# A transformer block on one core: the bound's root in a query and a key part, norms over the whole array, values transposed between score tiles

## The chip, the cores and the metric

The kernel runs on one core of a Trainium2 chip. The metric is the device time of one execution in microseconds (us); lower is better. The median of three runs of the kernel before is 1413.35 us, the runs lie between 1410.28 and 1417.75 us. Its profile comes from one more execution.

Five engines work side by side, each through its own instructions in order: TensorE (PE; PEld is its loading of weights), VectorE (DVE), ScalarE (ACT), GpSimd (POOL) and SyncE (SP), which here only issues DMAs. An engine that waits for a semaphore holds up everything that stands behind it in its own order.

## The reference

2048 tokens of width 512 go through a block of two parts: attention with 32 query heads of width 16, which share one key and one value head, and a gated feed-forward part of inner width 1792.

```python
def _A_ref(x, wq, wk, wv, wo):
    B, S, D = x.shape
    H = 32
    Dh = D // H
    q = (x @ wq).reshape(B, S, H, Dh).transpose(0, 2, 1, 3)
    k = x @ wk
    v = x @ wv
    scores = jnp.einsum("bhqd,bkd->bhqk", q, k) * (Dh ** -0.5)
    p = _softmax(scores, axis=-1)
    o = jnp.einsum("bhqk,bkd->bhqd", p, v)
    return o.transpose(0, 2, 1, 3).reshape(B, S, H * Dh) @ wo

def _B_ref(x, w_gate, w_up, w_down):
    return (_gelu(x @ w_gate) * (x @ w_up)) @ w_down

h = x + _A_ref(_layernorm(x), ...)
h2 = h + _B_ref(_layernorm(h), ...)
```

## The kernel before

The 2048 tokens are cut into four blocks of 512 (NB = 4, T = 512). Matrix products run in about full precision: each operand is split into a high and a low part, and three products (high by high, high by low, low by high) are added up.

**The prologue** (`prologue`, up to 50 us) normalizes the 16 tiles of 128 tokens, turns them on TensorE (`turn`), and projects keys and values of each block together (`project_k`, tiles pk). From a block's tile `add_k` writes the keys into `kaug`, `leave_k` copies the tile into SBUF as `vT`, `low_k` forms the keys' low part on GpSimd, `turn_v` transposes the values on TensorE (four transposes of 128x128, tile pv) and `leave_v` copies them into `v_sb` on VectorE. Beside that `project_q` projects the queries of block 0 in four chunks of 8 heads: chunk 0 in the generator `q_first`, chunks 1 to 3 in `q_rest`. Each chunk's tile pq is split into `qh` and `ql` (two buffers of each), and SP writes them to DRAM (`q_d`) in three DMAs, from where tiles of four heads (`qg`) are read.

**The bound.** In place of the row maximum the softmax subtracts a bound: with a head's query norms and the largest key norm, a line that lies above their product. `norm_k` sums the squares of a block's keys with a matmul against `ones`; `max_k` takes the largest; `k2m` is the maximum over the four blocks. `norm` does the same for the queries of a chunk with the matrix `sel`, with `q2` its largest value per head. `factors` makes the line's two coefficients out of q2 and k2m in four small GpSimd steps, ScalarE forms the tile `m` from them, and `first_bound` sends its rows into `qg_first` and to DRAM. The chunk for which this is urgent is chunk 0 of block 0.

**The steps.** Then the loop in `run` goes through score steps n. A step (`score`, `scores`) multiplies one block of 128 keys with the queries of two heads, a pair of matmuls into a PSUM tile s of two banks, and ScalarE takes the exponential of the whole tile. Two steps make one i of four heads; `finish` then weighs the values (`weigh`, four matmuls into acc). In the first steps three s tiles take six banks and acc one; the eighth bank is the only one left to `psum1` there (width = 1). From step START = 8 on, projections of the later query blocks are mixed in (line 429).

**What sets the order.** The pools and a hand-kept order: TensorE, ScalarE and GpSimd run in the order in which the code issues, and VectorE and SP do so in the prologue's end and in the steps. Behind step 2 the loop drains what is left of `q_rest`: for chunk 3 that is the split of the copy `pq_raw` into qh and ql on VectorE (lines 129 and 130), its square (line 265) and its three writes on SP (line 270). Its qh takes the buffer of chunk 1.

Lines of the profile that matter: L223 projection of block 0's queries, L242 the copy pq_raw, L280 norm of the queries, L290 to L299 the factors, L323 the tile m, L354 to L386 the DMAs of the first query tile and of m, L431 scores, L435 exponentials, L439 weighing, L1361 norm of the keys, L1387 the values' transposes, L1392 and L1393 their copies, L1464 k2m.

Of the kernel before, what the change touches and what calls it, by code (L numbers as in the profile page):

```python
# [9 lines left out]
F32 = mybir.dt.float32  # L10
# [20 lines left out]
W2 = 3  # L31

AHEAD_W = 2

LAST_Q = 258

# [26 lines left out]
def kernel(  # L63
# [104 lines left out]
    def run(outer, first):  # L168
# [37 lines left out]
        def project_q(b, cs, eng, col, whole=None):  # L206
# [68 lines left out]
                    yield 3  # L275

            def norm():
                pn = psum1(f"pqn_{b}_{cs[0]}")[:H, :]
                for i, c in enumerate(cs):
                    nc.tensor.matmul(  # L280
                        pn, sel[:, c, :], qss[i], start=(i == 0), stop=(i == len(cs) - 1)
                    )
                qn = eb.tile([H, T], F32, tag="qn", bufs=1, name=f"qn_{b}_{cs[0]}")
                nc.vector.tensor_copy(qn, pn)
                nc.vector.tensor_reduce(q2[:, col : col + 1], qn, axis=AX.X, op=ALU.max)

                mm = eb.tile([H, 3], F32, tag="mm", bufs=2, name=f"mm_{b}_{cs[0]}")

                def factors():
                    nc.gpsimd.tensor_scalar(  # L290
                        mm[:, 0:1], q2[:, col : col + 1], k2m, 1e-30, op0=ALU.mult, op1=ALU.add
                    )
                    nc.gpsimd.tensor_tensor(
                        mm[:, 1:2], mm[:, 0:1], power[:H, 0:1], op=ALU.pow
                    )
# [3 lines left out]
                    nc.gpsimd.tensor_scalar(  # L299
                        mm[:, 1:2], mm[:, 1:2], k2m, 0.5, op0=ALU.mult, op1=ALU.mult  # L300
                    )

                m = eb.tile([H, T], F32R, tag="m", bufs=2, name=f"m_{b}_{cs[0]}")

                def bound():
                    factors()
                    nc.gpsimd.tensor_scalar(
                        m, qn, mm[:, 1:2], mm[:, 2:3], op0=ALU.mult, op1=ALU.add
                    )
                    hs = slice(cs[0] * HC, (cs[-1] + 1) * HC)  # L310
                    nc.gpsimd.dma_start(q_d[hs, 3 * DH, tsl].bitcast(F32), m[hs].bitcast(F32))

                if not urgent:
                    after.append([2, bound])
                return qn, mm, m, factors

            if not urgent:
                norms.append(norm)
# [8 lines left out]


        after, squares, norms, pause = [], [], [], [0]
        ms = {}  # L330
# [64 lines left out]
        if first:  # L395
            set_banks("ps_pro")
            width = 8
            order = tc.manual_schedule(engines={mybir.EngineType.DVE})
            with order:
                qg_first = prologue(  # L400
                    psum1, xT, wq_hi, wq_lo, sel, k2m, q_first, q_rest, advance,
                    first_q, first_bound, fill_first, eb
                )
        sb = outer.enter_context(tc.tile_pool(name="attn", bufs=1, side="right"))
# [669 lines left out]
        with tc.manual_schedule(engines={mybir.EngineType.SP, mybir.EngineType.DVE}):  # L1074
# [6 lines left out]
            while n < lead:  # L1081
# [33 lines left out]
                for kind in kinds:  # L1115
                    if kind == "m" and not rest and not held and token not in (None, REST):
                        held = token[1] == 1
                        tokens = token, next(work)
                        score(n, [(lane, step) for lane, _, step in tokens])
                        token = next(work, None)  # L1120
                        left -= 2
                    else:
                        score(n)
                    n += 1
                if first and n == 2:
                    for _ in q_rest:
                        pass
# [117 lines left out]
        late.close()  # L1245


    def prologue(psum1, xT, wq_hi, wq_lo, sel, k2m, q_first, q_rest, advance, first_q, first_bound, fill_first, eb):
        with ExitStack() as pro:
            sb = pro.enter_context(tc.tile_pool(name="pro", bufs=1))  # L1250
            xT[0] = [sb.tile([P, DC, T], F32R, name=f"xT_{w}_0") for w in ("hi", "lo")]
# [25 lines left out]
            def repeat_k():  # L1277
# [17 lines left out]
                out=sel, in_=sel, compare_op=ALU.is_ge, fill=0.0, base=DH - 1,  # L1295
                pattern=[[-P, DC], [DH, H]], channel_multiplier=-1,
            )

            bias = sb.tile([P, 1], F32, name="bias")
            nc.vector.memset(bias, 0.0)  # L1300
# [1 line left out]
            nc.vector.memset(neg, -1.0)  # L1302
            for r0 in (0, 64):
                nc.scalar.dma_start(bias[r0 + 3 * DH : r0 + KR, :], neg)
            ones = sb.tile([DH, H], BF16, name="ones")
            nc.vector.memset(ones, 1.0)
            k2 = sb.tile([H, NB], F32, name="k2")
            nc.vector.memset(v_sb, 1.0)

# [42 lines left out]
                    )  # L1352

            def square_k(b, pk):
                ks = sb.tile([DH, T], BF16, tag="ks", bufs=2, name=f"ks_{b}")
                nc.scalar.activation(ks, pk[:DH, :], AF.Square)
                return ks

            def norm_k(b, ks):
                pn = psum1(f"pkn_{b}")[:H, :]  # L1360
                nc.tensor.matmul(pn, ones, ks, start=True, stop=True)  # L1361
                return pn

            def max_k(b, pn):
                nc.vector.tensor_reduce(k2[:, b : b + 1], pn, axis=AX.X, op=ALU.max)
# [100 lines left out]
            with tc.manual_schedule(engines={mybir.EngineType.SP}):  # L1466
# [100 lines left out]
```

## Time and profile before

| what | value |
|---|---|
| median of the runs | 1413.35 us |
| span of the profiled execution, first to last instruction | 1408.1 us |
| TensorE busy | 1391.7 us, 99% of the span |
| ScalarE busy | 1041.2 us, 74% |
| VectorE busy | 552.7 us, 39% |
| GpSimd busy | 189.4 us, 13% |
| mean granted TensorE clock | 0.996 |
| HBM read and written | 142.93 and 49.55 MB |

The profiled execution is known by its span; what lies around the span is not in the profile, and the runs were timed apart from it. The rows in the prediction come from these views: the page (span, busy time by engine), the busy time by stretches of the span with the granted clock (1.00 is full speed), the waits (who waited for whom), and the instructions of one engine in order of time. In the last, a row gives the start and the length in us, the engine and the source line, the operation, the written tile and the read ones, the shape, and the count of instructions merged into it; brackets hold the idle time ahead of it and what ended that. A merged row runs from its first start to its last end. Matmuls overlap in these rows, so that distances between starts tell the rate.

### The profile page before, as it was taken

The page shows a single profiled execution, that of the slowest core. Times are in us where ns is not written, and L with a number is a line of the kernel's source. Part 1 is how long each engine was busy: PE and PEld are TensorE (multiplying, and loading weights), DVE is VectorE, ACT ScalarE, POOL GpSimd, SP SyncE. Part 2 cuts the span into 40 slices and gives each one's busy share as a digit, 9 for nine tenths or more (in the row PEclk, how much of TensorE's full clock was granted, in tenths as well). Part 3 has the DMA queues.
Part 4 walks back from the last instruction along what each step waited for, and adds up shares of the span by engine and source line. Part 5 has one row for each costly group of instructions (what it writes and reads, how often), then busy time and mean ns, then how long its engine had stood idle before and what let it go on. Part 6 is the DMA issues. An engine that isn't in the chain of part 4 may idle for free.

```text
span 1408.1 us, 25648 instructions
## 1 busy us (share of the span) xinstructions
PE 1391.7 (99%) x10646; PEld 782.7 (56%) x10646; DVE 552.7 (39%) x982; ACT 1041.2 (74%) x1149; POOL 189.4 (13%) x288
## 2 busy tenths in 40 slices
PE   8999999999999999999999999999999999999998
PEld 7433333335555555555555655555555555557886
DVE  7322323333342434333252433424352342427665
ACT  7699999996777787777787777777787777772000
POOL 6655565501000000000000000001000000002000
PEclk9999999999999999999999999999999999999999
DMA  4578777842341322233252332223242241335551
GB/s 160 162 238 273 236 243 243 298 134 91 126 150 53 124 106 102 73 112 122 84 169 72 117 118 87 87 100 111 99 151 97 88 147 56 134 124 198 181 199 59
DMA packets 85041, 194.52 MB, mean 138 GB/s; under 512 B 9904, under 2 KB 24240, under 8 KB 84884
## 3 DMA queue, kind: packets, MB, share of 16 engines
q1 hardware_dynamic: 77484, 167.39, 35.3%
q0 software_dynamic: 7264, 25.30, 5.0%
q8 instruction: 86, 1.41, 0.4%
q14 instruction: 39, 0.32, 0.1%
q10 hardware_dynamic: 168, 0.10, 0.0%
HBM read 142.93 MB, written 49.55 MB: 137 GB/s over the span
## 4 chain that ended last, share of the span: by engine, by line
PE 93%; ACT 3%; DMA 1%; issue 1%; DVE 1%; POOL 0%; SPq 0%; ACTq 0%; DVEq 0%; POOLq 0%
PE acc L439 33%; PE s L431 19%; PE pu L949 9%; PE pg L949 8%; PE pd L949 4%; PE pq L429 4%; PE pd L626 3%; ACT p L435 3%; PE pd L648 3%; PE pg L648 3%; PE pu L648 3%; PE pp L626 2%; PE pp L757 1%; DMA x<-in_A_x_dram 1%; PE pxt L693 1%
## 5 line engine op out<-in xcount | busy, mean ns | idle before, releaser
L435 ACT ACTIVATE p<-s 128x1024 f32<-128x1024 f32 x1024 | 969.7, 1030 | 224.6 <-PE s L431 220.1
L439 PE MATMUL acc<-p,v_sb 128*32 128x512 f32 x4096 | 496.4, 600 | 0.0
L431 PE MATMUL s<-qg,kaug 50*128 50x512 f32 x1984 | 416.3, 423 | 3.7 <-ACT p L435 3.6
L431 PEld LDWEIGHTS s<-qg,kaug 50*128 50x128 f32 x1984 | 194.6, 184 | 217.8 <-ACT p L435 120.6
L439 PEld LDWEIGHTS acc<-p,v_sb 128*32 128x32 f32 x4096 | 109.8, 109 | 229.2 <-issue 226.0
L949 PE MATMUL pu<-x2h,w 64*128 64x512 f32 x672 | 211.8, 391 | 0.0
L949 PE MATMUL pg<-x2h,w 64*128 64x512 f32 x672 | 211.5, 391 | 0.1
L949 PEld LDWEIGHTS pu<-x2h,w 64*128 64x128 f32 x672 | 115.8, 185 | 15.1
L949 PEld LDWEIGHTS pg<-x2h,w 64*128 64x128 f32 x672 | 116.2, 185 | 12.6 <-DVE g L823 0.5
L949 PE MATMUL pg<-x2l,w 64*128 64x512 f32 x336 | 122.2, 391 | 0.0
L949 PE MATMUL pu<-x2l,w 64*128 64x512 f32 x336 | 121.8, 390 | 0.0
L826 ACT ACTIVATE ga<-ga 128x512 f32<-128x512 f32 x56 | 35.3, 634 | 89.2 <-DVE ga L821 89.2
L139 POOL TENSOR_SCALAR rstd<-mv 128x1 f32<-128x1 f32 x16 | 3.5, 221 | 666.4 <-DVE mv L137 666.4
L949 PE MATMUL pd<-w,gh 64*128 64x512 f32 x384 | 81.3, 392 | 0.0
L891 DVE TENSOR_TENSOR h<-h,pd 128x512 f32<-128x512 f32 x48 | 31.9, 685 | 115.4 <-PE pd L949 66.4
L1192 DVE SCALAR_TENSOR_TENSOR ga<-ga,g 128x512 f32<-128x512 f32 x70 | 48.3, 691 | 52.3 <-ACT ga L826 51.2
L452 DVE COPY oT<-acc 128x512 f32<-128x512 f32 x32 | 22.1, 692 | 112.1 <-PE acc L439 111.9
L479 DVE RECIPROCAL oc<-oc 128x128 f32<-128x128 f32 x64 | 56.3, 921 | 24.3 <-DMA oc<-acc_d 19.5
L810 DVE COPY g<-pg 128x512 f32<-128x512 f32 x56 | 38.8, 692 | 62.8 <-PE pg L949 57.0
L949 PEld LDWEIGHTS pu<-x2l,w 64*128 64x128 f32 x336 | 57.9, 185 | 7.6
L949 PEld LDWEIGHTS pg<-x2l,w 64*128 64x128 f32 x336 | 58.1, 185 | 6.1
L823 DVE SCALAR_TENSOR_TENSOR g<-g,pu 128x512 f32<-128x512 f32 x56 | 38.2, 683 | 40.4 <-PE pu L949 30.4
(248 smaller groups left out, 1462.4 us busy)
## 6 DMA issues: line engine op xcount, KB each, us to landing
w<-w_d SPq DMA_DIRECT2D x112, 512.0 KB
w<-w_d SPq DMA_DIRECT2D x28, 1024.0 KB
qg<-q_d SPq DMA_DIRECT2D x46, 200.0 KB
q_d<-qh SPq DMA_DIRECT2D x32, 256.0 KB
wo<-wo_d SPq DMA_DIRECT2D x8, 1024.0 KB
acc_d<-oT SPq DMA_DIRECT2D x31, 256.0 KB
oc<-acc_d SPq DMA_DIRECT2D x124, 64.0 KB
w_d<-w_0b POOLq DMA_DIRECT2D x14, 512.0 KB, 7.6
```

The lines of the kernel that those rows point to most:

```text
L429: step()
L431: nc.tensor.matmul(s[:, a, :], kaug[rows, kc * P : (kc + 1) * P], qg[rows, 2 * u + a, :], start=True, stop=True,)
L435: nc.scalar.activation(p[:, 2 * u : 2 * u + 2, :], s, AF.Exp, scale=SCALE)
L439: nc.tensor.matmul(acc[32 * j : 32 * j + 32, :], v_sb[:, kc, :], p[:, j, :], start=(kc == 0), stop=(kc == KC - 1), skip_group_check=True,)
L479: nc.vector.reciprocal(oc[:, 1, sl], oc[:, 1, sl])
L626: nc.tensor.matmul(banks[k], lhsT[rows], rhs[rows], start=(turn == 0 and i == 0), stop=(turn == 1 and i == n - 1), skip_group_check=True,)
L648: nc.tensor.matmul(bank, lhsT, rhs, start=(i == 0), stop=(i == len(ts) - 1))
L810: nc.vector.tensor_copy(g, pg)
L823: nc.vector.scalar_tensor_tensor(g, g, 0.5, pu, op0=ALU.mult, op1=ALU.mult)
L826: nc.scalar.activation(a, a, AF.Tanh, scale=GELU_A * GELU_C)
L949: nc.tensor.matmul(e["bank"], lhsT[rows], rhs[rows], start=i == 0 and not e["both"], stop=last and e["both"], skip_group_check=True,)
L1192: (soon or lazy).pop(0)()
```

## The change

Four things are changed, all in the prologue and the first steps.

The root of the urgent bound is split: `norm` computes the query part (`ab`: half the root, and half its inverse, of q2) on GpSimd as soon as q2 is there; `first_factors` then needs of k2m only its root, on GpSimd, and one product on VectorE.

The norms' matmuls of the prologue use all 128 columns and rows: `ones` becomes a 128x128 matrix with zeros behind the first 16 rows, the keys' squares are taken over all 128 rows, and the urgent query norm multiplies with a new 128x128 matrix `wide` (the first chunk's columns of `sel`, zeros elsewhere). The results are read from the same 32 partitions.

The values of blocks 2 and 3 are no longer transposed in the prologue, but behind steps 3 and 4 of the loop (TURN_V), into the bank of `psum1`.

Behind steps 2, 5 and 6 (BUSY) stand three matmuls each whose results nobody reads, into the same bank.

```diff
+TURN_V = {3: 2, 4: 3}
+
+BUSY = (2, 5, 6)
...
             def norm():
-                pn = psum1(f"pqn_{b}_{cs[0]}")[:H, :]
+                pn = psum1(f"pqn_{b}_{cs[0]}")
                 for i, c in enumerate(cs):
                     nc.tensor.matmul(
-                        pn, sel[:, c, :], qss[i], start=(i == 0), stop=(i == len(cs) - 1)
-                    )
+                        pn if urgent else pn[:H, :], wide[0] if urgent else sel[:, c, :],
+                        qss[i], start=(i == 0), stop=(i == len(cs) - 1),
+                    )
+                pn = pn[:H, :]
...
+                if urgent:
+                    ab = eb.tile([H, 2], F32, name="ab")
+                    nc.gpsimd.tensor_scalar(
+                        mm[:, 0:1], q2[:, col : col + 1], 1e-30, None, op0=ALU.add
+                    )
+                    nc.gpsimd.tensor_tensor(
+                        ab[:, 0:1], mm[:, 0:1], power[:H, 0:1], op=ALU.pow
+                    )
+                    nc.gpsimd.tensor_scalar(
+                        ab[:, 1:2], mm[:, 0:1], ab[:, 0:1], 0.5, op0=ALU.mult, op1=ALU.mult
+                    )
+                    nc.gpsimd.tensor_scalar(ab[:, 0:1], ab[:, 0:1], 0.5, None, op0=ALU.mult)
+
+                def first_factors():
+                    nc.gpsimd.tensor_tensor(mm[:, 0:1], k2m, power[:H, 1:2], op=ALU.pow)
+                    nc.vector.tensor_scalar(mm[:, 1:3], ab, mm[:, 0:1], None, op0=ALU.mult)
...
+                    if first and n in TURN_V:
+                        turn_last(TURN_V[n])
+                    if first and n in BUSY:
+                        bank = psum1(f"busy_{n}")
+                        for _ in range(3):
+                            nc.tensor.matmul(
+                                bank, kaug[:KR, :P], cur["qg"][:KR, 0, :],
+                                start=True, stop=True,
+                            )
...
+            wide.append(sb.tile([P, P], BF16, name="wide"))
+            nc.gpsimd.memset(wide[0], 0.0)
+            nc.gpsimd.tensor_copy(wide[0][:, :H], sel[:, 0, :])
...
-            ones = sb.tile([DH, H], BF16, name="ones")
-            nc.vector.memset(ones, 1.0)
+            ones = sb.tile([P, P], BF16, name="ones")
+            nc.vector.memset(ones, 0.0)
+            nc.vector.memset(ones[:DH], 1.0)
...
-                ks = sb.tile([DH, T], BF16, tag="ks", bufs=2, name=f"ks_{b}")
-                nc.scalar.activation(ks, pk[:DH, :], AF.Square)
+                ks = sb.tile([P, T], BF16, tag="ks", bufs=2, name=f"ks_{b}")
+                nc.scalar.activation(ks, pk, AF.Square)
...
                 advance(q_rest, 12)
-                for b in range(1, NB):
-                    leave_v(b, turn_v(b, vTs[b]))
+                leave_v(1, turn_v(1, vTs[1]))
                 advance(q_rest, 3 * DC * (DC - FIRST_Q) - 21)
-            return qg
+            return qg, lambda b: leave_v(b, turn_v(b, vTs[b]))
```

On TensorE, from the end of the queries' projection (pq) to the first mixed one, the score pairs (s), the weighing (acc) and the last of the projection stand before as follows; the three groups pv ahead of them are the transposes of blocks 1, 2 and 3.

```order
L1387 MATMUL pv_748<-ident,vT_651 128x128 x4
L1387 MATMUL pv_755<-ident,vT_688 128x128 x4
L1387 MATMUL pv_762<-ident,vT_691 128x128 x4
...
L431 MATMUL s_0_816<-qg_first,kaug 128x512 x2
L431 MATMUL s_1_820<-qg_first,kaug 128x512 x2
L431 MATMUL s_0_834<-qg_first,kaug 128x512 x2
L431 MATMUL s_1_838<-qg_first,kaug 128x512 x2
L431 MATMUL s_0_846<-qg_first,kaug 128x512 x2
L431 MATMUL s_1_850<-qg_first,kaug 128x512 x2
L439 MATMUL acc_0_814<-p_815,v_sb 32x512 x4
```

The same place of TensorE now, from the first score pair to the first weighing:

```order
L453 MATMUL s_0_809<-qg_first,kaug 128x512 x2
L453 MATMUL s_1_813<-qg_first,kaug 128x512 x2
L1152 MATMUL busy_817<-qg_first,kaug 128x512 x3
L453 MATMUL s_0_831<-qg_first,kaug 128x512 x2
L1422 MATMUL pv_835<-ident,vT_697 128x128 x4
L453 MATMUL s_1_842<-qg_first,kaug 128x512 x2
L1422 MATMUL pv_846<-ident,vT_700 128x128 x4
L453 MATMUL s_0_857<-qg_first,kaug 128x512 x2
L1152 MATMUL busy_861<-qg_first,kaug 128x512 x3
L453 MATMUL s_1_865<-qg_first,kaug 128x512 x2
L1152 MATMUL busy_869<-qg_first,kaug 128x512 x3
L461 MATMUL acc_0_807<-p_808,v_sb 32x512 x4
```

The transposes of blocks 2 (pv_835) and 3 (pv_846) moved behind the third and the fourth score pair, and nine matmuls (busy) were added.

On VectorE, before, the copies of the values (v_sb) of blocks 1, 2 and 3 stand together, ahead of the splits of query chunks 2 (ql_2) and 3 (qh_3, ql_3, qs_3):

```order
L1392 COPY v_sb<-pv_748 128x4x14
L1393 COPY v_sb<-pv_748 128x4x2
L1392 COPY v_sb<-pv_755 128x4x14
L1393 COPY v_sb<-pv_755 128x4x2
L1392 COPY v_sb<-pv_762 128x4x14
L1393 COPY v_sb<-pv_762 128x4x2
L130 TENSOR_TENSOR ql_2_773<-pq_2_738,qh_2_772 128x512
L265 TENSOR_TENSOR qs_2_776<-qh_2_772 128x512
L129 CAST qh_3_824<-pq_raw_3_794 128x512
L130 TENSOR_TENSOR ql_3_825<-pq_raw_3_794,qh_3_824 128x512
L265 TENSOR_TENSOR qs_3_828<-qh_3_824 128x512
```

The same place of VectorE now:

```order
L1427 COPY v_sb<-pv_755 128x4x14
L1428 COPY v_sb<-pv_755 128x4x2
L134 TENSOR_TENSOR ql_2_766<-pq_2_745,qh_2_765 128x512
L269 TENSOR_TENSOR qs_2_769<-qh_2_765 128x512
L133 CAST qh_3_821<-pq_raw_3_787 128x512
L134 TENSOR_TENSOR ql_3_822<-pq_raw_3_787,qh_3_821 128x512
L269 TENSOR_TENSOR qs_3_825<-qh_3_821 128x512
L1427 COPY v_sb<-pv_835 128x4x14
L1428 COPY v_sb<-pv_835 128x4x2
L1427 COPY v_sb<-pv_846 128x4x14
L1428 COPY v_sb<-pv_846 128x4x2
```

The copies of blocks 2 and 3 moved behind the split of query chunk 3.

More of the change, by code (lines that the diff above doesn't have):

```diff
@@ L314, in norm @@
                     after.append([2, bound])
-                return qn, mm, m, factors
+                return qn, mm, m, first_factors if urgent else factors
             if not urgent:
@@ L329, in run @@
         after, squares, norms, pause = [], [], [], [0]
-        ms = {}
+        ms, wide = {}, []
         q_first = project_q(0, range(FIRST_Q), nc.scalar, 0)
@@ L399, in run @@
             with order:
-                qg_first = prologue(
-                    psum1, xT, wq_hi, wq_lo, sel, k2m, q_first, q_rest, advance,
+                qg_first, turn_last = prologue(
+                    psum1, xT, wq_hi, wq_lo, sel, k2m, wide, q_first, q_rest, advance,
                     first_q, first_bound, fill_first, eb
@@ L1245, in run, with prologue @@
         late.close()
-    def prologue(psum1, xT, wq_hi, wq_lo, sel, k2m, q_first, q_rest, advance, first_q, first_bound, fill_first, eb):
+    def prologue(psum1, xT, wq_hi, wq_lo, sel, k2m, wide, q_first, q_rest, advance, first_q, first_bound, fill_first, eb):
         with ExitStack() as pro:
@@ L1354, in square_k @@
             def square_k(b, pk):
-                ks = sb.tile([DH, T], BF16, tag="ks", bufs=2, name=f"ks_{b}")
-                nc.scalar.activation(ks, pk[:DH, :], AF.Square)
+                ks = sb.tile([P, T], BF16, tag="ks", bufs=2, name=f"ks_{b}")
+                nc.scalar.activation(ks, pk, AF.Square)
                 return ks
             def norm_k(b, ks):
-                pn = psum1(f"pkn_{b}")[:H, :]
+                pn = psum1(f"pkn_{b}")
                 nc.tensor.matmul(pn, ones, ks, start=True, stop=True)
-                return pn
+                return pn[:H, :]
             def max_k(b, pn):
```

## The prediction

> **What bounds the kernel now.** I read the page, then busy time by stretches around the clock's dips, then each engine in order of time between 35 and 62 us. The page first:
>
> ```profile
> span 1408.1 us, 25648 instructions
> PE 1391.7 (99%) x10646; PEld 782.7 (56%) x10646; DVE 552.7 (39%) x982; ACT 1041.2 (74%) x1149; POOL 189.4 (13%) x288
> ```
>
> TensorE is busy in 99% of the span. What the change can win or lose lies in the few stretches where it waits or where its clock is low. In busy time by stretches, the columns are the length, the busy time of PE, PEld, DVE, ACT and POOL, then the granted clock, the DMA share and GB/s:
>
> ```profile
> 49.94:53.35 3.41, 1.93 (x10) 0.79 (x8) 0.00 (x0) 2.21 (x3) 3.35 (x7) 1.00 0.67 188
> 53.35:56.76 3.41, 2.91 (x12) 0.77 (x12) 0.00 (x0) 3.41 (x5) 3.26 (x3) 0.50 0.54 170
> 56.76:60.17 3.41, 3.41 (x16) 0.70 (x12) 1.72 (x3) 2.52 (x3) 2.55 (x4) 0.50 0.52 190
> 60.24:310.00 249.76, 249.67 (x1891) 93.81 (x1887) 71.32 (x101) 244.55 (x263) 127.46 (x162) 1.00 0.75 241
> 310.00:1395.00 1085.00, 1080.79 (x8440) 644.74 (x8437) 438.71 (x786) 755.73 (x824) 21.70 (x44) 1.00 0.33 115
> ```
>
> In 49.94 to 53.35 us TensorE worked 1.93 of 3.41 us, and for the next 6.82 us it was granted half its clock. From 60.24 us it has full clock and 0.09 us of idle in 250 us. So an instruction that comes some microseconds later at 60 us is still as late at 310 us. Behind 310 us the idle is 4.2 us in all, and its waits are of this kind (engine, line, what it waited for, us in total, times, longest):
>
> ```profile
> PE s L431 <- ACT p L435: 3.6, 14, 0.4
> ```
>
> These 14 waits are for ScalarE, which follows TensorE; they move along and absorb nothing. I therefore take a shift at 60.24 us, where the first mixed projection starts, to reach the end in full. TensorE around the place (start, length, line, operands, count, idle before):
>
> ```profile
> 45.36 1.47 PE L1387 MATMUL pv<-ident,vT 128*128 128x128 f32 x12
> 48.31 0.40 PE L223 MATMUL pq<-xT_lo,wq_hi 128*128 128x512 f32 x1
> 48.54 0.39 PE L223 MATMUL pq<-xT_hi,wq_lo 128*128 128x512 f32 x1
> 49.94 0.39 PE L223 MATMUL pq<-xT_hi,wq_lo 128*128 128x512 f32 x1
> 51.08 1.03 PE L431 MATMUL s<-qg_first,kaug 50*128 50x512 f32 x6 [0.75 <-ACT pq_raw L242]
> 52.81 0.50 PE L431 MATMUL s<-qg_first,kaug 50*128 50x512 f32 x2 [0.70 <-ACT p L435]
> 53.73 1.71 PE L431 MATMUL s<-qg_first,kaug 50*128 50x512 f32 x4 [0.41 <-ACT p L435]
> 55.37 1.93 PE L439 MATMUL acc<-p,v_sb 128*32 128x512 f32 x8
> 57.23 1.22 PE L431 MATMUL s<-qg_first,kaug 50*128 50x512 f32 x4
> 58.38 1.93 PE L439 MATMUL acc<-p,v_sb 128*32 128x512 f32 x8
> 60.24 0.50 PE L429 MATMUL pq<-xT_hi,wq_hi 64*128 64x512 f32 x1
> ```
>
> Three gaps (0.75, 0.70, 0.41 us) precede and accompany the dip. ScalarE in the same time:
>
> ```profile
> 45.78 0.81 ACT L323 ACTIVATE m<-qn,mm 32x512 fp32r<-32x512 f32 x1 [2.00 <-POOL mm L299]
> 50.43 0.60 ACT L242 ACTIVATE pq_raw<-pq 128x512 f32<-128x512 f32 x1 [1.86 <-PE pq L223]
> 51.73 5.61 ACT L435 ACTIVATE p<-s 128x1024 f32<-128x1024 f32 x6 [0.71 <-PE s L431]
> 61.02 11.37 ACT L435 ACTIVATE p<-s 128x1024 f32<-128x1024 f32 x12 [1.01 <-PE s L431]
> ```
>
> The first score tile waits for the copy pq_raw, which ends at 51.03 us. An exponential takes 0.94 us (5.61 over 6).
>
> **The start (memsets, the wide matrix).** GpSimd gets a memset and a small copy behind its selects:
>
> ```profile
> 1.82 0.31 POOL L1294 TENSOR_SCALAR_AFFINE_SELECT sel<-sel 128x128 bf16<-128x128 bf16 x1
> 5.11 0.23 POOL L1320 TENSOR_SCALAR rstd<-mv 128x1 f32<-128x1 f32 x1 [2.97 <-DVE mv L1318]
> ```
>
> A wait of 2.97 us covers both; without that cover they would cost two operations of about 0.3 us. VectorE's one extra memset comes to 0.1 us at most; I take nothing.
>
> **Norms in whole-array form.** Five matmuls get 128 columns of weights for 32, and the key squares 128 rows for 16. The weight loads (idle before in brackets):
>
> ```profile
> 35.90 0.09 PEld L1361 LDWEIGHTS <-ones 16*32 16x32 bf16 x1 [0.17 <-issue]
> 36.21 0.19 PEld L1349 LDWEIGHTS pk<-xT_hi,wk_hi 128*128 128x128 f32 x1 [0.23 <-issue]
> ```
>
> Between a 32-column load (0.09 us) and a 128-column one (0.19 us) lies 0.1 us, so five cost 0 to 0.5 us; a gain is excluded as no work goes away. TensorE is busy without a gap from here to 50.34 us, so this would count on the way to the first score. I take 0.4 us, near the 128-column row.
>
> **The root in two parts.** GpSimd's old chain and VectorE's inputs to it:
>
> ```profile
> 43.80 0.26 POOL L290 TENSOR_SCALAR mm<-q,k2m 32x1 f32<-32x1 f32 x1 [6.66 <-DVE k2m L1464]
> 44.13 0.54 POOL L293 TENSOR_TENSOR mm<-mm,power 32x1 f32<-32x1 f32 x1
> 45.12 0.62 POOL L299 TENSOR_SCALAR mm<-mm,k2m 32x1 f32<-32x1 f32 x1
> 42.07 0.67 DVE L285 TENSOR_REDUCE q<-qn 32x1 f32<-32x512 f32 x1
> 43.55 0.14 DVE L1464 TENSOR_SCALAR k2m<-k2m 32x1 f32<-32x1 f32 x1
> 43.62 0.67 DVE L129 CAST qh<-pq 128x512 fp32r<-128x512 f32 x1
> ```
>
> Before, four steps ran behind k2m, 43.80 to 45.74 us. Now four start behind the query maximum (42.74 us) and take 1.0 us for scale and root and about 0.7 for the two small ones: to 44.45 us. Then come the key's root (0.54) and one VectorE product (0.14), so m can start at 45.3 instead of 45.78 us: 0.5 us earlier. VectorE waits in that product for GpSimd's root, and the split of query chunk 1, queued behind it, starts near 45.25 instead of 43.62 us and ends near 47.2 us (three operations of 0.67). SP fetches that chunk only behind the rows of m:
>
> ```profile
> 46.62 1.49 SPq L381 DMA_DIRECT2D qg_first<-m  x2
> 48.71 0.68 SPq L270 DMA_DIRECT2D q_d<-qh  x1
> 50.20 2.05 SPq L270 DMA_DIRECT2D q_d<-qh  x2
> ```
>
> SP reaches it at 48.71 us, so the slip is hidden. The 0.5 us gained on m is about what the norms lose, so I leave SP's writes where they are; the bounds are 0.5 us earlier and unchanged.
>
> **Two transposes moved, nine matmuls added.** Eight transposes of 0.12 us leave the stretch before the first score, which therefore starts near 50.5 us (51.08 less 1.0, plus 0.4). Blocks 2 and 3 are now transposed behind the third and fourth score pair. There only one PSUM bank is left for such tiles: the dummies and both transposes share it. The transposes of block 3 must wait until VectorE has copied out block 2, and that copy now stands behind the split of query chunk 3. VectorE's rows:
>
> ```profile
> 46.00 0.22 DVE L1392 COPY v_sb<-pv 128x56 f32<-128x56 f32 x1 [0.38 <-PE pv L1387]
> 46.13 0.16 DVE L1393 COPY v_sb<-pv 128x8 f32<-128x8 f32 x1
> 58.29 0.43 DVE L129 CAST qh<-pq_raw 128x512 fp32r<-128x512 f32 x1 [8.41 <-DMA q_d<-qh]
> 59.36 0.69 DVE L265 TENSOR_TENSOR qs<-qh 128x512 bf16<-128x512 f32 x1
> ```
>
> The split reuses the buffer of chunk 1 and waits 8.41 us for SP's write of it, issued at 50.20, to land at 58.29 us. Before, nobody waited for that. Now TensorE does: after the fourth score pair, near 53.2 us, it stands in order at block 3's transposes with every later score, dummy and weighing behind it.
>
> The sum, step by step:
> - VectorE is free of the split at 60.05 us (59.36 + 0.69), the two copies take 0.29 (46.00 to 46.29): bank free 60.34, TensorE goes on at 60.4.
> - TensorE idles some 7 us, more than in the stretch that halved the clock before, so it restarts at half clock.
> - Work left ahead of the first mixed projection, at half clock: four transposes 2 x 0.49 = 0.98; four score pairs at 0.61 (1.22 over 2) = 2.44; six dummies at 2 x 0.23 (48.31 to 48.54) = 2.76; two weighings at 1.93 = 3.86. Together 10.04 us, or 5.02 at full clock.
> - The clock came back at 60.17 us behind a stretch of 3.41 us in which TensorE never paused, and had not come back behind one with 2.91 of 3.41. One full stretch behind 60.4 us ends between 63.8 and 67.2 us, by where its edge falls. Work done at T + (10.04 - (T - 60.4))/2: 67.1 to 68.8 us.
> - Against 60.24 us that is 6.9 to 8.6 us later; the middle is 7.7. Landing 0.5 us earlier takes off 0.25.
>
> The Trainium skill, "TensorE: Matmul & The Clock Gate", Part 1, has a free-running window of about 3.4 us and lets one busy window restore the clock; an estimate by it alone gives the same 3.4 to 6.8 us of half clock after the restart. Its table of practical rules allows pauses up to about 3 us without a loss. The trace differs there: the pauses of at most 0.75 us at 50 to 54 us were followed by half clock. By that rule dummies of this kind would buy nothing here; by the rows they might, but the stall of 7 us is beyond either.
>
> Scale: the profiled execution gives its span, 1408.1 us; the median of the runs, 1413.35, lies 5.25 above it, which is what lies around the span and the scatter (1410.28 to 1417.75). I add the difference of spans to the median: 1413.35 + 7.7 = 1421.0 us. About 0.5% (7.1 us) is what a measurement of this kernel can tell from no change.
>
> **The rivals.**
> - *The bank is free in time (not slower).* If block 2's copies were done by 53.2 us, for which chunk 1's write would have to land by 51 us, TensorE would need from 50.5 us eight pairs at 0.34 (1.03 over 3), nine dummies at 0.23, eight transposes at 0.12 and two weighings at half of 1.93: 7.7 us, to 58.2, and the exponentials 0.6 + 8 x 0.94 = 8.1, to 58.6 against 61.02. Gain 2.0 to 2.4, say 2.2: 1411.1 us. For it: the clock would not dip. Against it: the landing at 58.29. Chance 0.10.
> - *The write lands about 2 us earlier.* It shares the DMA engines (share 0.54 in that stretch) with other transfers that also shift. Restart at 58.4: 2 x 0.5 = 1 us less with the same clock edges, up to 2 with earlier ones: about +6, 1419.4 us. Chance 0.15.
> - *The clock does not return while the work lasts.* If one full stretch is not enough after a long pause, all 10.04 us run at half clock: 70.4, that is +10.2, 1423.6 us. For it: the 2.91 us stretch did not suffice. It decides where the stretch behind 63.6 us is still at 0.50. Chance 0.15.
>
> **How the numbers follow.** My forecast has 0.60. Its own range (6.5 to 8.6) straddles 7.1 us, and medians scatter by some 2 us, so about 0.6 of it is slower by over 0.5%. Slower: 0.36 + 0.14 of the third rival + 0.03 of the second = 0.53. Faster: 0.03, scatter on top of the first rival. Same: 0.44. The range runs from 1416.0, where the second rival ends with its scatter, to 1425.0, where the third does; the first rival and the tails are left out.
>
> **What would show it.** Right: VectorE's split of chunk 3 still begins near 58 us behind a write; TensorE has one idle stretch of 6 to 7 us ahead of a transpose that waits for the value copy; the clock is 0.50 for 3 to 7 us after 60; the first mixed projection is near 68 us, and the shift is unchanged at 310 us. Wrong: no idle above 1 us behind the fourth pair (first rival), the split at 56 us (second), or a first mixed projection beyond 69.5 (third). A shift at 68 us that shrinks later would break the step that carries it to the end.

## The result and the profile after

| kernel | median of the runs | range | profiled span |
|---|---|---|---|
| before, same chip | 1412.54 us (6 runs) | 1410.28 to 1417.75 | 1408.1 us |
| after | 1420.62 us (6 runs) | 1419.36 to 1422.75 | 1419.0 us |

The ratio after to before is 1.0064, with a 95% interval of 1.005 to 1.0077: slower by 0.64%. (The ratios of this document are estimated from the runs; the quotient of the two medians alone can differ by up to 0.001, here 1.0057.) 1421.0 us was forecast.

TensorE after, around the first steps, in order of time:

```profile
44.34 0.60 PE L1422 MATMUL pv<-ident,vT 128*128 128x128 f32 x4
...
49.43 0.60 PE L453 MATMUL s<-qg_first,kaug 50*128 50x512 f32 x2 [1.00 <-DVE ql L134]
51.18 0.50 PE L453 MATMUL s<-qg_first,kaug 50*128 50x512 f32 x2 [1.15 <-DMA qg_first<-m]
...
53.53 0.80 PE L453 MATMUL s<-qg_first,kaug 50*128 50x512 f32 x2
59.82 1.09 PE L1422 MATMUL pv<-ident,vT 128*128 128x128 f32 x4 [5.50 <-DVE v_sb L1428]
60.84 0.79 PE L453 MATMUL s<-qg_first,kaug 50*128 50x512 f32 x2
...
69.51 0.58 PE L451 MATMUL pq<-xT_hi,wq_hi 64*128 64x512 f32 x1
```

The one long wait is the predicted one: 5.50 us ahead of block 3's transposes, ended by VectorE's copy of the values. Two shorter ones, of 1.00 and 1.15 us, stand ahead of the first two score pairs. The first mixed projection starts at 69.51 us, 9.27 us behind the 60.24 of before. VectorE after shows the queue in which that copy stood:

```profile
43.02 0.14 DVE L1499 TENSOR_SCALAR k2m<-k2m 32x1 f32<-32x1 f32 x1
44.39 1.34 DVE L309 TENSOR_SCALAR mm<-ab,mm 32x2 f32<-32x2 f32 x1 [1.23 <-POOL mm L308]
...
57.72 0.43 DVE L133 CAST qh<-pq_raw 128x512 fp32r<-128x512 f32 x1 [7.79 <-DMA q_d<-qh]
58.18 0.69 DVE L134 TENSOR_TENSOR ql<-pq_raw,qh 128x512 fp32r<-128x512 f32 x1
58.79 0.68 DVE L269 TENSOR_TENSOR qs<-qh 128x512 bf16<-128x512 f32 x1
59.39 0.21 DVE L1427 COPY v_sb<-pv 128x56 f32<-128x56 f32 x1
59.51 0.16 DVE L1428 COPY v_sb<-pv 128x8 f32<-128x8 f32 x1
```

The split of chunk 3 waits 7.79 us for the write of chunk 1, and the two copies, whose transposes had ended at 53.60 us (52.54 + 1.06), come behind it. Busy time by stretches after, cut where the clock changes and every 3.41 us between:

```profile
49.23:52.64 3.41, 2.06 (x10) 1.26 (x11) 0.69 (x2) 1.92 (x2) 3.35 (x6) 1.00 0.61 154
52.64:56.05 3.41, 1.68 (x6) 0.84 (x6) 0.00 (x0) 2.07 (x3) 3.18 (x4) 0.50 0.50 162
56.05:59.47 3.42, 0.00 (x0) 0.00 (x0) 1.72 (x4) 0.00 (x0) 1.77 (x3) 0.50 0.64 221
59.47:62.88 3.41, 3.06 (x11) 2.15 (x11) 0.49 (x4) 1.02 (x1) 0.03 (x1) 0.50 0.61 208
62.88:66.29 3.41, 3.41 (x13) 1.03 (x11) 0.00 (x0) 1.02 (x1) 3.03 (x4) 0.50 0.64 211
66.30:69.71 3.41, 3.41 (x18) 0.90 (x16) 0.00 (x0) 1.94 (x2) 1.85 (x3) 0.50 1.02 252
69.71:310.00 240.29, 240.19 (x1823) 90.91 (x1823) 61.96 (x95) 235.40 (x253) 119.42 (x150) 1.00 0.72 234
```

Half clock lasts from 52.64 to 69.71 us, 17.07 us. It begins behind the two short waits, and 1.68 us ahead of the stall, which runs from 54.32 to 59.82 us. After the stall two stretches in which TensorE never paused passed before full clock came back, where before one had been enough. Behind 69.71 us TensorE idles 0.1 us in 240 us. Compared exponential by exponential, the shift against before is +9.3 us from the ninth on, to 308 us, and +9.15 at 475 to 600 us; at 719 us of after 1.7 us more come from one wait that before did not have (engine, line, what it waited for, us in total, times, longest):

```profile
PE pu L971 <- DMA w<-w_d: 1.3, 1, 1.3
```

### The profile page after: what moved, and what is told of

It reads as the page before. It is cut to its first block, busy times and chain, and to the rows that moved or that the text cites. A ratio compares the mean times of both kernels' runs of the same rounds, so it can differ in the third digit from the quotient of the medians.

```text
span 1419.0 us, 25671 instructions
## 1 busy us (share of the span) xinstructions
PE 1394.9 (98%) x10655; PEld 784.1 (55%) x10655; DVE 547.1 (39%) x984; ACT 1041.3 (73%) x1149; POOL 189.3 (13%) x291
## 4 chain that ended last, share of the span: by engine, by line
PE 91%; ACT 3%; DMA 2%; DVE 1%; issue 1%; POOL 0%; SPq 0%; ACTq 0%; DVEq 0%; POOLq 0%
PE acc L461 33%; PE s L453 19%; PE pu L971 9%; PE pg L971 7%; PE pd L971 4%; PE pq L451 4%; PE pd L648 3%; PE pd L670 3%; PE pg L670 3%; PE pu L670 3%; ACT p L457 3%; PE pp L648 2%; PE pp L779 1%; PE pxt L715 1%; DMA q_d<-qh 1%
## 5 line engine op out<-in xcount | busy, mean ns | idle before, releaser
L832 DVE COPY g<-pg 128x512 f32<-128x512 f32 x56 | 38.7, 692 | 63.4 <-PE pg L971 57.6
```

The costliest lines, as they stand in the source:

```text
L832: nc.vector.tensor_copy(g, pg)
```

## The experiments

Each was timed beside the kernel before on the same chip; differences are against that median. "First mixed" is the start of the first mixed projection in the profiled execution (60.24 us before, 69.51 after).

| run | median, us | before | ratio, 95% interval | first mixed, us |
|---|---|---|---|---|
| transposes moved, nothing else | 1417.12 | 1410.84 | 1.0047, 1.0033 to 1.006 | 67.83 |
| after, transposes back in the prologue | 1412.78 | 1410.84 | 1.0009, 0.9996 to 1.0022 | 57.70 |
| after, value copies ahead of chunk 3's split | 1415.28 | 1410.84 | 1.0032, 1.002 to 1.0044 | 64.43 |
| after, no dummies | 1416.03 | 1410.84 | 1.0039, 1.0025 to 1.0053 | 65.68 |
| after, stall filled with matmuls | 1417.68 | 1410.41 | 1.005, 1.0037 to 1.0063 | 67.30 |
| copies first, 128-row dummies | 1416.21 | 1410.41 | 1.004, 1.0027 to 1.0053 | 60.05 |
| copies first, product on GpSimd | 1411.31 | 1410.41 | 1.0006, 0.9995 to 1.0018 | 57.58 |
| root and norms alone | 1409.91 | 1410.41 | 0.9998, 0.9989 to 1.0007 | 57.00 |
| copies first, product on GpSimd, query loads earlier | 1409.71 | 1410.55 | 1.0002, 0.9988 to 1.0016 | 57.60 |
| the same without dummies | 1409.33 | 1410.55 | 0.9987, 0.9978 to 0.9995 | 56.03 |
| copies first, product on GpSimd, no dummies | 1412.34 | 1410.55 | 1.0007, 0.9995 to 1.0018 | 56.03 |
| before, query loads earlier | 1411.41 | 1410.55 | 1.0006, 0.9996 to 1.0016 | 60.26 |

The theory: the moved transposes wait for a bank that VectorE frees late; the wait and the half clock behind it make the whole loss. The rivals: the dummies make it, or the other parts of the change do.

### Is it the moved transposes?

The first run takes from the change only TURN_V with `turn_last`, on the kernel before.

> The kernel before with one part of the change alone: the transposes of the values of blocks 2 and 3 moved behind score steps 3 and 4. Theory (one PSUM bank, its release queued on VectorE behind the split of query chunk 3): TensorE idles 5 to 7 us ahead of block 3's transposes until VectorE's copy near 60 us, the clock goes to half, and the kernel is 6 to 9 us slower than before, 1418.5 to 1421.5. Rival (the nine added matmuls, the wider norms or the split root cost the time): no idle stretch above 1 us there and 1411 to 1414, as before.

TensorE of that kernel:

```profile
50.22 1.03 PE L433 MATMUL s<-qg_first,kaug 50*128 50x512 f32 x6 [0.75 <-ACT pq_raw L244]
60.79 1.09 PE L1391 MATMUL pv<-ident,vT 128*128 128x128 f32 x4 [8.34 <-DVE v_sb L1397]
67.83 0.79 PE L431 MATMUL pq<-xT_hi,wq_hi 64*128 64x512 f32 x1
```

The stall is there without the other parts, 8.34 us long, and costs 6.3 us: the theory's mechanism, at some 1.4 us less than the lower end expected. The counterpart puts the transposes back and keeps all else:

```diff
-TURN_V = {3: 2, 4: 3}
+TURN_V = {}
...
-                leave_v(1, turn_v(1, vTs[1]))
+                for b in range(1, NB):
+                    leave_v(b, turn_v(b, vTs[b]))
```

> The changed kernel with the transposes of all blocks back in the prologue; root, wide norms and the nine added matmuls stay. Theory: the stall of 5.5 us is gone, and the added matmuls fill part of the pauses between the first scores: 1409.5 to 1413. Rival (the added matmuls, norms or root cost the time): 1418 or more, with the clock at half for more than 7 us.

No stall and full clock in the first steps; the first mixed projection starts 2.54 us earlier than before. Still the kernel isn't faster: what it had won was lost again between 200 and 242 us (below). The third run leaves the change whole and only drains `q_rest` later, so that the copies stand ahead of chunk 3's split:

```diff
-                if first and n == 2:
+                if first and n == 4:
                     for _ in q_rest:
```

> The changed kernel with one order changed: the split of query chunk 3 is issued behind step 4 instead of step 2, so that VectorE copies the values of blocks 2 and 3 out ahead of it. Nothing else is touched; the single bank stays. Theory: VectorE's copies follow TensorE's transposes within 1 us, no idle above 1 us behind the fourth score pair, first mixed projection near 58 to 60 us, 1409.5 to 1412. Rival (TensorE is held by something else, or the clock falls in any case): the first mixed projection stays beyond 66 us, 1418 or more.

The expectation missed. The copies are done at 54.43 and 56.15 us and the stall is gone, yet the clock is half for 13.65 us. The first two score pairs of that kernel, then its busy time by stretches:

```profile
49.44 0.59 PE L453 MATMUL s<-qg_first,kaug 50*128 50x512 f32 x2 [0.99 <-DVE ql L134]
51.40 0.50 PE L453 MATMUL s<-qg_first,kaug 50*128 50x512 f32 x2 [1.37 <-DMA qg_first<-m]
```

```profile
49.09:52.50 3.41, 1.69 (x9) 1.16 (x9) 0.85 (x2) 1.61 (x3) 3.35 (x6) 1.00 0.57 158
52.50:55.91 3.41, 3.41 (x14) 1.88 (x12) 0.34 (x3) 2.54 (x3) 3.19 (x4) 0.50 0.46 151
55.91:59.32 3.41, 3.41 (x10) 2.13 (x10) 0.66 (x3) 1.96 (x2) 1.93 (x3) 0.50 0.60 179
59.32:62.74 3.42, 3.42 (x17) 0.88 (x20) 1.31 (x3) 0.57 (x2) 0.00 (x0) 0.50 0.67 232
62.74:66.15 3.41, 3.41 (x16) 1.45 (x14) 0.00 (x0) 1.91 (x3) 1.89 (x2) 0.50 0.59 181
```

Two waits of 0.99 us (for VectorE's split) and 1.37 us (for the DMA of m) leave 1.69 of 3.41 us busy, and the clock falls; four stretches without a pause follow before it returns. So the stall is one cause of the loss, and a fall of the clock behind the short waits at the first two score pairs is another; the run with the product on GpSimd, below, takes these waits away. They do not bring the fall each time: in the profiled execution of the run with 128-row dummies, waits of 1.00 and 1.16 us at the same place were followed by none.

### What the clock and the dummies do

The next run drops the dummies from the change (BUSY = ()).

> The changed kernel without the nine added matmuls. Theory: the stall stays (about 5.5 to 6.5 us ahead of block 3's transposes), but of the work at half clock behind it 2.8 us fall away: 1.4 to 2.8 us less than the changed kernel, 1417.5 to 1419.5. Rival (the added matmuls are the cost): back to 1411 to 1414.

The stall stays (5.26 us), and the time is 5.2 us above before, where the change is 8.1: by these medians, taken at different times, the nine dummies cost about 3 us, a little more than the 1.4 to 2.8 expected. In the traces the first mixed projection starts at 65.68 against 69.51 us, 3.83 us earlier: the expectation had counted the dummies' own 2.8 us at half clock, but the half clock also ends a stretch sooner, after 13.65 instead of 17.07 us. The next keeps the dummies and gives TensorE matmuls to do in the stall; they write to acc before it is first used:

```diff
+                    if first and n == 4:
+                        for _ in range(FILL):
+                            nc.tensor.matmul(
+                                acc, kaug[:, :P], kaug[:, :T],
+                                start=True, stop=True, skip_group_check=True,
+                            )
```

> The changed kernel with the stall filled: 14 matmuls over the whole array, whose results are written over later, stand ahead of block 3's transposes. The wait for VectorE's copy stays. Theory (half of the loss is the clock that the wait leaves at half): the transposes still start near 59.8 us, the clock is back at full by 60 us, the work behind takes about 5 us instead of 9.7, first mixed projection near 65 instead of 69.5 us, 1415 to 1417. Rival (the wait alone is the cost, or the clock does not follow what TensorE does): 1419 to 1422.

Block 3's transposes run at 60.18 us with full clock, but between 59.60 and 63.01 us 0.63 us of pauses are followed by a second fall, and the first mixed projection comes at 67.30, not at 65 us. The median, 1417.68 us, lies between the ranges of the theory and of the rival, and its interval overlaps that of the change itself (1.0037 to 1.0063 against 1.005 to 1.0077). By the trace half clock makes part of the loss, and the release at 60 us stays; how large that part is, the medians do not tell. The last run of this group makes the dummies 128 rows high, on the kernel with copies first:

```diff
-                                bank, kaug[:KR, :P], cur["qg"][:KR, 0, :],
-                                start=True, stop=True,
+                                bank, kaug[:, :P], kaug[:, :T], start=True, stop=True,
```

> The order of the copies-first run (no stall), with the nine added matmuls over all 128 rows of the array instead of 50. There the clock was at half from 52.5 to 66.2 us although TensorE did not pause from 51.4 us on. Theory C (what counts for the clock is how much of the array works): with 128 rows the clock comes back one or two stretches of 3.41 us earlier, by 59.3 or 62.7, and the time falls by 1 to 3 us to 1412 to 1414. Theory D (only pauses count): the clock stays at half until about 66 us and the time near 1415.

This run was inconclusive. Its profiled execution took 1410.41 us and shows no half clock at the start; its four others took 1414.69 to 1416.64 us. Whether the rows of a matmul count for the clock stays open.

### What the root and the norms are worth

The product moves from VectorE to GpSimd, on the kernel with copies first:

```diff
-                    nc.vector.tensor_scalar(mm[:, 1:3], ab, mm[:, 0:1], None, op0=ALU.mult)
+                    nc.gpsimd.tensor_scalar(mm[:, 1:3], ab, mm[:, 0:1], None, op0=ALU.mult)
```

> The order of the run before last (chunk 3's split behind the value copies), and the product of the split root on GpSimd instead of VectorE. In the changed kernel that product took 1.34 us on VectorE, to the moment when GpSimd ended the first of two key subtractions that it had begun meanwhile. Theory A (VectorE's product is blocked by GpSimd's subtraction): on GpSimd it takes 0.2 to 0.4 us, m starts 0.8 to 1.1 us earlier (near 44.8), the rows of m land as much earlier, and the idle ahead of the first two score pairs falls from 2.4 to about 1.4 us or less; 3 to 5 us less than with the order alone, 1410 to 1412. Theory B (the product is slow by its own form): it takes over 1 us on GpSimd too, and the time stays near 1415.

GpSimd, ScalarE and the first score pairs on TensorE, of that kernel:

```profile
43.78 0.56 POOL L308 TENSOR_TENSOR mm<-k2m,power 32x1 f32<-32x1 f32 x1
44.45 0.79 POOL L309 TENSOR_SCALAR mm<-ab,mm 32x2 f32<-32x2 f32 x1
45.31 2.63 POOL L1414 TENSOR_TENSOR kaug<-vT,kaug 16x512 fp32r<-16x512 f32 x2
```

```profile
45.27 0.81 ACT L345 ACTIVATE m<-qn,mm 32x512 fp32r<-32x512 f32 x1 [1.91 <-POOL mm L309]
```

```profile
49.16 0.81 PE L453 MATMUL s<-qg_first,kaug 50*128 50x512 f32 x4 [0.75 <-ACT pq_raw L246]
```

m starts at 45.27 us, 0.5 us earlier than before and after (45.78 and 45.76), where 0.8 to 1.1 were expected: the product took 0.79 us on GpSimd, between the 0.2 to 0.4 us of theory A and the more than 1 us of theory B. The waits for VectorE's split and for the DMA of m are gone, one of 0.75 us for ScalarE's copy is left, the clock stays full in the first steps, and the time is 1411.31 us (ratio 1.0006), where the kernel with copies first had 1415.28 (1.0032). The run with root and norms alone (no moved transposes, no dummies) keeps the product on VectorE:

> The change without the moved transposes and without the nine matmuls: the split root and the wide norms alone. Theory (the wide norms and the root cancel, since the product on VectorE ends no earlier than the old chain): first score pair at 50 to 51.2 us, m starts within 0.3 us of 45.8, the clock at half for about 7 us as before, 1410 to 1413, no difference. Rival (root and norms hold a part of the loss): 1414 or more.

Its product takes 1.33 us, m starts at 45.75 us, and yet the first mixed projection comes at 57.00 us, 3.24 us earlier than before: the norms' gain, told below, and a clock that did not fall in these steps, where half clock for about 7 us was expected. It is not kept either. TensorE's waits of this kernel from 60 to 310 us:

```profile
PE s L453 <- DMA qg<-q_d: 3.6, 3, 1.4
```

Before has no such wait in this stretch.

### Where the gain at the start goes

Three kernels were 2.5 to 3.2 us ahead at 57 us and no faster in the end: after with the transposes back, copies first with the product on GpSimd, and root and norms alone. Their profiled executions took 1415.40, 1413.44 and 1413.03 us, 2.1 to 3.1 us above their medians, so that these traces show more of the loss than a median execution has. SP, before and in the kernel with root and norms alone, ahead of one load of query tiles:

```profile
184.67 0.37 SPq L535 DMA_DIRECT2D w_1r<-in_B_w_up_dram  x1
185.14 0.46 SPq L456 DMA_DIRECT2D acc_d<-oT  x1
185.69 1.13 SPq L411 DMA_DIRECT2D qg<-q_d  x2
```

```profile
190.31 0.37 SPq L557 DMA_DIRECT2D w_1r<-in_B_w_up_dram  x1
190.78 0.46 SPq L478 DMA_DIRECT2D acc_d<-oT  x1
191.32 0.98 SPq L433 DMA_DIRECT2D qg<-q_d  x2
```

The load goes out 5.6 us later while TensorE needs it some 3 us sooner. On SP it stands behind a load of raw weights, which waits for a buffer that GpSimd has to empty; and GpSimd waits for its own writes of split weights to land. GpSimd's largest such wait from 60 to 310 us, before and in that kernel:

```profile
POOL w_0b L129 <- DMA w_d<-w_1b: 12.8, 6, 4.3
```

```profile
POOL w_0b L133 <- DMA w_d<-w_1b: 17.9, 8, 5.4
```

This sum alone does not explain the lateness: in the other two kernels it is 11.5 and 14.7 us. What the three share comes earlier, at the first piece of w_1, before and with root and norms alone:

```profile
84.34 0.62 POOL L129 CAST w_1b<-w_1r 128x512 fp32r<-128x512 f32 x1
```

```profile
90.14 0.60 POOL L133 CAST w_1b<-w_1r 128x512 fp32r<-128x512 f32 x1 [4.08 <-DMA wo_d<-wo3b]
```

In all three GpSimd waits there 4.1 to 4.6 us for a write of the weights wo, which before does not, begins the piece 5.3 to 5.8 us later than before, and is still about 5 to 6 us late at 190 us. Why that write lands later is not shown.

To test it, the loads of query groups 3 to 7 are asked for two key tiles earlier, on the kernel with copies first and the product on GpSimd:

```diff
-                if kc == 2 and b * NG + g + 1 < NB * NG:
+                early_q = first and b == 0 and 2 <= g < NG - 1
+                if kc == (0 if early_q else 2) and b * NG + g + 1 < NB * NG:
```

> The kernel with copies first and the product on GpSimd, and the loads of query groups 3 to 7 of block 0 asked for two key tiles (about 4 us) earlier. Theory (what the start gains is given back near 203 and 236 us because these loads land 1.3 to 1.5 us late): no wait of TensorE for a query tile above 0.5 us before 310 us, no low clock there, the shift of -2.7 us still there at 310 us, 1407.5-1409.5 us beside 1410.5 of before. Rival (the transfers as a whole are the limit there; an earlier request only moves the lateness to the next transfer): another wait of 1 us or more between 140 and 310 us, 1410.5-1412 us.

Both had a part of it; the median, 1409.71 us, lies between their ranges. Busy time by stretches of that kernel:

```profile
51.00:290.00 239.00, 238.82 (x1805) 91.30 (x1807) 64.80 (x97) 234.11 (x252) 132.69 (x165) 1.00 0.75 245
293.23:296.64 3.41, 1.29 (x7) 0.61 (x7) 1.12 (x3) 1.30 (x2) 0.00 (x0) 1.00 0.70 238
296.64:300.05 3.41, 3.41 (x15) 0.86 (x19) 0.69 (x1) 2.03 (x3) 0.00 (x0) 0.50 0.45 144
```

To 290 us there is no wait, and the lead over before is still 2.65 us at 240 us. Then the two transfers of the next query tile, whose load was not moved, come late (1.47 and 0.66 us), the clock falls, and the lead is gone: the lateness moved to the next load, as the rival had it. This profiled execution took 1413.40 us, 3.7 above the kernel's median. The last three runs:

> The same without the nine dummy matmuls. If they are what keeps the clock up in the first steps: a low clock near 52 us and a first mixed projection near 62 us instead of 57.6, 1412-1414 us. If the clock would have stayed up without them (as with the root and the norms alone): they cost at most their own 2 us where TensorE and not ScalarE is the limit, 1407-1409.5 us.

> Copies first, product on GpSimd, no dummy matmuls, query loads as in before. Same question as in the run before it: low clock near 52 us and 1413-1416 us if the dummies hold the clock, 1410-1411.5 us if not.

> The kernel before with only the query loads asked for earlier. Both theories: before has no wait above 0.1 us there, so no gain, 1410-1411.5 us; under the rival a loss of up to 1 us is possible.

Without dummies the clock stays full in the first steps in both kernels, and their first mixed projection comes at 56.03 us against 57.6 with dummies: where nothing stalls, the dummies hold no clock up and cost 1.6 us there. Between the two only the time of the query loads differs, and they were timed together: 1409.33 us with the earlier loads and 1412.34 without, so that these loads are worth some 3 us to a kernel that is ahead; the second missed its range (1410 to 1411.5) by 0.8 us. The first is the only kernel below before with its whole interval (0.9987, 0.9978 to 0.9995), by less than 2 us, and in its profiled execution (1410.60 us, the longest of its eleven) it too loses its lead, at 293 to 299 us; the other gives its lead back at 205 to 266 us. Before with earlier loads shows no gain, as expected.

## Why the prediction was right, and where it was off

**The stall: right.** One bank, the copy queued behind chunk 3's split, the split behind SP's write: each link stands in the rows of after. The copies end at 59.67 us (59.51 + 0.16), where 60.34 was worked out, and the moved transposes alone bring it about. The stall's length was less right: 5.50 us and not 6 to 7. The prediction let the score pairs run from 50.5 us without a wait, to a fourth pair that ends near 53.2 us; they waited 1.00 and 1.15 us, the clock fell at 52.64 us, and the fourth pair ended at 54.32 us. The clock was thus at half before the stall, and not through it, as the sum's second step had it. With the transposes alone (8.34 us of stall) it fell during the stall. Neither changes when the stall ends.

**The clock's return: mis-sized.** The step "One full stretch behind 60.4 us ends between 63.8 and 67.2 us" failed: the clock came back at 69.71 us, behind two full stretches (62.88 to 69.71), 2.5 us beyond the later edge. By the prediction's own mark (69.5 us) this is the third rival's outcome, to which it gave 0.15: all the work between the stall and the first mixed projection ran at half clock, +9.27 us against 6.9 to 8.6 forecast and +10.2 for that rival. Of the 0.9 us between, 0.6 is the earlier restart, at 59.82 and not 60.4 us, and the rest the work itself, 9.69 us and not 10.04.

**The norms: the sign was wrong.** The step "a gain is excluded as no work goes away" failed. TensorE's weight loads after, at the place of the two rows shown of before:

```profile
36.13 0.10 PEld L1396 LDWEIGHTS <-ones 128*128 128x128 bf16 x1
36.24 0.19 PEld L1384 LDWEIGHTS pk<-xT_hi,wk_hi 128*128 128x128 f32 x1
```

Before, the small load was preceded by 0.17 us without a load and the next one came 0.31 us behind it; now there is no such gap and the distance is 0.11 us. The load of 128 columns is also hardly longer than the small one's (0.10 against 0.09 us); the 0.19 that stood for it belongs to f32 weights. Over the stretch with five norms TensorE gained 1.46 us, 0.28 to 0.30 at each: from the first value transposes to the next it took 8.53 us (35.81 to 44.34) and 9.99 before. The rows before for that:

```profile
35.37 0.60 PE L1387 MATMUL pv<-ident,vT 128*128 128x128 f32 x4
```

The first score pair therefore started at 49.43 us, not near 50.5; the stall swallowed all of it.

**The root: mis-sized, without effect on the end.** The product took 1.34 us, not 0.14, and m gained nothing, though the query maximum, from which the chain starts, was there 0.54 us earlier (42.20 against 42.74 us). GpSimd after:

```profile
43.79 0.56 POOL L308 TENSOR_TENSOR mm<-k2m,power 32x1 f32<-32x1 f32 x1
44.43 2.63 POOL L1414 TENSOR_TENSOR kaug<-vT,kaug 16x512 fp32r<-16x512 f32 x2
```

The product (44.39 to 45.73 us) lasts just as long as the first of the two subtractions beside it (44.43, half of 2.63: to 45.75). With the product on GpSimd m comes 0.5 us earlier. That this is the gain that the prediction had priced is luck: the earlier query maximum, a gain of the norms that it had excluded, makes up for the 0.65 us by which the product is longer than the 0.14 it had put down.

**The shift is carried to the end: right for a delay.** +9.3 us were still there at 308 us; the 1.7 us at 719 us are beside it. For a gain the same sentence would have been false, as the kernels that were ahead at 57 us show. The first rival's 1411.1 us rested on it; the two kernels that came nearest to it, copies first with the product on GpSimd, took 1411.31 us with dummies and 1412.34 without.

**The scale: two errors against each other.** That the forecast lies within 0.4 us of the median is luck; the mechanism was right, the terms were not. Between the profiled executions the difference is 10.9 us (1419.0 less 1408.1), 3.2 more than the 7.7 forecast: 1.6 at the first mixed projection, by the clock less the earlier restart, and the rest by the late wait at 719 us. The timed run of after's profiled execution took 1420.73 us, 1.7 above its span; before's, by the same 1.7, took about 1409.8 us, 3.5 below the median of 1413.35 that the sum started from. I had called those 5.25 us "what lies around the span and the scatter"; most of it was scatter. The six runs of before in the result are few: its medians in the experiments, of 16 to 35 runs, are 1410.41 to 1410.84 us, and against those the change costs about 10 us, though they were taken at other times and on other chips.

## What to carry to other kernels

Before moving work behind a point where only one buffer is left, read what stands in the queue of the engine that empties the buffer: here a copy of 0.29 us stood behind a wait of 7.8 us for a DMA. A delay ahead of a stretch in which nothing idles is carried to its end; a gain is carried only if every transfer into the stretch can come as much earlier, which the waits of before do not show, since none is late yet. Small operations in a chain are priced beside what the other engines run at that moment, not by the shortest row of their kind.

## What the runs showed of the hardware

**Small weight tiles.** Between whole-array matmuls, a norm in the 16x32 form (one of the five: 128x32) cost TensorE about 0.29 us more than in the 128x128 form (1.46 us over five). In the rows the loads around the small one come with gaps (0.17 us ahead, 0.31 us to the next load's start, against 0.11).

**VectorE beside GpSimd.** A 32x2 product took 1.34 and 1.33 us on VectorE when a GpSimd subtraction of 1.32 us began beside it, and 0.79 us on GpSimd. The Trainium skill, "SBUF — State Buffer", section "Who interferes with whom", describes a port pair that GpSimd shares with VectorE in its two-port modes, and that whoever issues first holds for a whole instruction while the other is blocked. The ends at 45.73 and 45.75 us agree with it; the starts do not, as VectorE began first in the trace (44.39 against 44.43 us). No run has this product on VectorE without a subtraction beside it, so the cause is argued and not shown. VectorE's cast out of PSUM at 45.65 us took its usual 0.67 us beside the second subtraction.

**The clock.** All half-clock times up to 310 us were multiples of 3.41 us. Twelve returns were seen: eight behind one stretch in which TensorE never paused, three behind two, one behind four. The twelve falls followed stretches with 0.75 to 2.78 us busy of 3.41; but a stretch of 2.37 us (56.18 to 59.60, filled stall) was followed by none, and neither were 2.00 of 3.40 us around 234 us (copies first, product on GpSimd, no dummies). Before with earlier query loads runs the same program as before up to there, and its half clock lasted 10.24 us (53.78 to 64.02), where before's had 6.83. So busy time by stretches does not decide it alone, and what does stays open. The Trainium skill, "TensorE: Matmul & The Clock Gate", Part 1, has one busy window of about 3.4 us restore the clock: eight of twelve agree, four do not. Its table of practical rules asks only that pauses stay under about 3 us; that is not enough here: most of these falls came behind waits of 0.2 to 1.5 us each.
